# Batch 1 of a sparse attention with an MoE layer behind it: values of pairs 2 and 3 loaded ahead of rows of k and q, one stage for all block sums, and ScalarE's front reordered

## The chip, the cores and the metric

The kernel runs on one core of one Trainium2 chip. The metric is the device time of one execution in microseconds; lower is better. Inputs and output are float32 in device memory.

## The reference, cut to what matters

```python
B, H, S, D = 4, 8, 768, 64;  block, window = 32, 16;  nb = S // block   # 24 blocks
scale = 1 / sqrt(D)
k_sum = k.reshape(B, H, nb, block, D).max(axis=3)
v_sum = v.reshape(B, H, nb, block, D).mean(axis=3)
scores_l = scale * q @ k.T                      # masked to |i - j| < window
scores_s = scale * q @ k_sum.T + log(block)
a = softmax(concat([masked scores_l, scores_s]))
attn = a @ concat([v, v_sum])
x = attn.transpose(0, 2, 1, 3).reshape(B * S, H * D)          # 3072 x 512
h = x @ w_in                                                  # 512 -> 2048
out = (h / (1 + exp(-beta * h))) @ w_out                      # 2048 -> 512
```

Each query sees its neighbours at less than 16 positions, and one key and one value for each of the 24 blocks: the block's maximum of k and its mean of v.

## The kernel before, in words

**Tiles.** The eight heads go in four pairs, g = 0 to 3. Queries are taken in tiles of 64, two to a chunk of 128 rows (par 0 and 1), six chunks to a sequence. For a pair, `kw` holds the turned keys (for par 1 a copy shifted by 64) with the 24 block maxima in the columns from 96 on, `qt` the turned queries. `ve` holds the values shifted by 16 rows for par 0, `vo` the same values shifted by 64 more for par 1; the lowest 96 partitions of each are values, the upper 32 block means. One matmul thus gives the scores of a tile with its neighbours and all blocks; the scores are exponentiated on ScalarE (`attn`), multiplied with a band of ones on VectorE (`mask`), and multiplied with `ve` or `vo` on TensorE (`av`). A column of ones in the values gives the sum, by which VectorE divides (`norm`). The result is turned (`x_transpose`) into `xT`.

**The layer behind.** Units of tokens go through `h_group` (matmuls with `w_in` of k1 = 4 steps, then Silu with the scale beta on ScalarE) and `o_part` (matmuls with `w_out`, copied out by ScalarE, written by SyncE). Batch 0 is two units of 384 tokens, each later batch is one of 768.

**Order.** There is no planner with costs: each engine runs its instructions in the order in which the program issues them. Batch 0's attention is written out by hand and comes first (the front). Then, for each batch b, the list `main` holds the h groups and the output parts of batch b with times (1.3 and 0.865 each), and `side` holds the steps of attention of batch b + 1 with times given by `at_time`; `side` is sorted by time and merged into `main`. `up` is the time at which the output parts begin. The times only give an order.

**Loads.** GpSimd issues all loads from device memory, converting to bf16, in one queue: k and q of batch 0, its values, w_in, `load_run` of k and q of pairs 0 and 1 of batch 1, w_out (four parts), values of batch 1. Pairs 2 and 3 of batch 1 are loaded as rows (`load_row`: four DMAs for a pair) and turned by `cross`, two DMA transposes for a pair on SyncE's queue. Pairs 0 and 1 are turned on TensorE (`prep_k`, `prep_q`). `load_v(1, 2, 2)` and `load_v_edge(1, True)` bring the values of pairs 2 and 3. Each load there waits until the eighth load before it has landed.

**The gate.** Batch 2's loads (`load_next`) are issued on GpSimd behind `open_gate`, a memset of one small tile first by VectorE, then by GpSimd, which so waits until VectorE has come to that place.

**Block means.** `mean_v` sums the values with the matrix `A_avg` on TensorE: nine steps, each with one matmul for each pair, into 32 partitions per pair (`vm_ps`). A cast takes the sums to `vm` (in batch 0 to `vm_first`, on ScalarE), and `rows_v` spreads them on VectorE over the upper partitions of `ve` and `vo`. `copy_v` makes `vo` from `ve` by DMA on SyncE's queue or by a copy on VectorE or ScalarE.

**The front.** `av_first` multiplies the first half of a pair's scores with values (L412) and then with `vm_first` (L419). `fill` and `keep_warm` are matmuls without use on a bank of TensorE's; the bank `big` of the front also holds the turned beta, which `beta_copy` reads (L237). `fill_band` makes half of the band on ScalarE (L221); `x0` turns half of x, copied by ScalarE (L481). The activation of one element into `spare` (L614) brings ScalarE's table for Silu.

Lines of the profile: L341 block sums, L345 and L348 their casts, L354 `rows_v`, L329 `copy_v`, L303 and L305 the DMA transposes of `cross`, L311 and L313 batch 2's block maxima, L438 scores, L443 masks, L456 `av`, L465 and L466 `norm`, L501 and L508 the h groups, L522 output parts.

Of the kernel before, what the change touches and what calls it, by code (L numbers as in the profile page):

```python
# [12 lines left out]
def kernel(  # L13
# [10 lines left out]
    nc = tc.nc  # L24
# [5 lines left out]
    ACTF = mybir.ActivationFunctionType  # L30

    B, H, S, D = q.shape
# [4 lines left out]
    nch = S // P  # L37
# [36 lines left out]
    HM = nch // 2  # L74
# [39 lines left out]
    def load_v(b, g, n=1):  # L114
        lo, hi = PC * g + 1, min(PC * (g + n) + 1, HC)
        rows = v[b].rearrange("h s d -> (h s) d")
        src = rows[lo * P - W:hi * P - W].rearrange("(c p) d -> p c d", p=P)
        nc.gpsimd.dma_start(out=ve_bufs[b % 2][:, lo:hi, 0:D], in_=src)  # L118

    def load_v_edge(b, last):  # L120
        ve = ve_bufs[b % 2]
        rows = v[b].rearrange("h s d -> (h s) d")
        if last:
            nc.gpsimd.dma_start(out=ve[0:W, HC, 0:D], in_=rows[H * S - W:H * S])
        else:
            nc.gpsimd.dma_start(out=ve[W:P, 0, 0:D], in_=rows[0:P - W])
# [18 lines left out]
    warm = const.tile([P, 512], bf16, name="warm")  # L145
    spare = const.tile([P, 1], f32, name="spare")
# [71 lines left out]
    def fill_band(m0, m1):  # L218

        for par in range(2):  # L220
            nc.scalar.copy(out=band[:, par, m0:m1].rearrange("p m h f -> p (m h) f"),  # L221
                           in_=near[:, None].to_broadcast([P, 2 * (m1 - m0), QT]))
# [26 lines left out]
    def load_w_out(i, c=k2 // 4):  # L249
        nc.gpsimd.dma_start(out=w_out_sb[:, i * c:(i + 1) * c], in_=w_out_r[:, i * c:(i + 1) * c])  # L250
# [3 lines left out]
    at = {}  # L254
# [67 lines left out]
    def copy_v(b, g, m0=0, m1=nch, copy=None):  # L322
        ve = ve_bufs[b % 2][:, PC * g:PC * (g + 1) + 1]
        vo = vo_bufs[b % 2][:, PC * g:PC * (g + 1)]
        copies = copy if isinstance(copy, tuple) else (copy or nc.sync.dma_start,) * 2
        for (lo, n, at, d), move in zip(((D, D, 0, 0), (0, 32, D, 1)), copies):
            dst = vo[at:at + n].rearrange("p (h c) e -> p h c e", h=2)[:, :, m0:m1]
            src = ve[lo:lo + n, d:PC + d].rearrange("p (h c) e -> p h c e", h=2)[:, :, m0:m1]
            move(out=dst, in_=src)  # L329

    def fill(t, n):
        for _ in range(n):
# [237 lines left out]
    load_v_edge(1, False)  # L570
    load_v(1, 0, 2)
    load_w_out(3)
    for g in (2, 3):
        load_row("k", 1, g)
        load_row("q", 1, g)
    load_v(1, 2, 2)
    load_v_edge(1, True)

    for g in range(npair):
        open_scores(g, 0)  # L580
# [14 lines left out]
    for g in range(2):  # L595
        copy_v(0, g, 0, HM, dve)
        copy_v(0, g, HM, nch)
    mean_v(0, (0, 1), "t", act)
    av_first(0)()
    norm((0, 0, 0), HM)  # L600
    av_first(1, ps.tile([P, 2, 512], f32, name="av_ps", tag="big", bufs=3))()
    norm((0, 1, 0), HM)
    fill(big, 1)
    beta_copy()
    fill_band(HM, nch)
    x0(0, act)
    copy_v(0, 2, 0, HM, dve)
    copy_v(0, 3, 0, HM, (act, dve))
    for g in (2, 3):
        copy_v(0, g, HM, nch)  # L610
    fill(big, 1)
    mean_v(0, (2, 3), "big", act)
    x0(1, act)
    nc.scalar.activation(out=spare[:], in_=warm[:, 0:1], func=ACTF.Silu)  # L614
    av_first(2)()
    norm((0, 2, 0), HM)
    av_first(3, ps.tile([P, 2, 512], f32, name="av_ps", tag="big", bufs=3))()
# [12 lines left out]
    for b in range(B):  # L630
        us = [u for u, z in enumerate(units) if z[0] == b]
        up = sum(NG[u] for u in us) * GT
        total = up + nch * 4 * OT
        nxt = b + 1 if b + 1 < B else None
        pairs = tuple(range(npair))
        side = []

        def at_time(t, f, *a):
            side.append((t, lambda: f(*a)))

        if b == 0:
            for g in pairs:
                t = 2.0 + 2.0 * g
                at_time(t - 1.4, mask_half, g)
                at_time(t - 1.4, rows_v, 0, g, HM, nch)
                at_time(t, av, (0, g, 1), HM, HM, "t")
                at_time(t, norm, (0, g, 1), HM)
                at_time(t + 1.9, x_transpose, (0, g, 1), HM, HM, "t", dve)
            at_time(7.0, fill_band, 0, HM)
            at_time(7.0, band_edge, False)  # L650
            for n in range(k2):
                at_time(up - 7.5 + 0.4 * n, scale_w_out, n)
        if nxt == 1:
            first, step = up + 0.3, 4.4
            for g in pairs:
                t = first + step * g
                p = (up - 9.0, up - 4.5, up + 7.5, up + 8.6)[g]
                if g < 2:
                    at_time(p, prep_k, 1, g, "t")
                    at_time(p + 0.8, prep_q, 1, g, "t", dve)  # L660
                    at_time(p + 0.8, copy_v, 1, g)
                else:
                    at_time(up + 0.5, cross, 1, g)
                    at_time(up + 6.1 if g == 2 else first + step * 2 + 0.1, copy_v, 1, g, 0, nch, act)
                at_time(p, top_k, 1, g)
                at_time(p if g < 3 else first + step * 2 + 0.7, rows_k, 1, g)
                for par in range(2):
                    at_time(t, scores, 1, g, par)
                    at_time(t, mask, 1, g, par)
                if g % 2 == 0:  # L670
                    m = up + 1.0 if g == 0 else first + step * 2 + 0.5
                    at_time(m, mean_v, 1, (g, g + 1), "big")
                    for i in (g, g + 1):

                        at_time(m if i < 3 else first + step * 2 + 0.8, rows_v, 1, i)
                a = t + 3.5
                at_time(a, av, (1, g), 0, nch)
                at_time(a, norm, (1, g), nch)
                at_time(a + (0.1 if g < 2 else 2.9), x_transpose, (1, g), 0, nch, "big", dve)
        elif nxt is not None:  # L680
            for g in pairs:
                t = (0.65, 1.95, 5.85, 9.75)[g]
                at_time(0.1, copy_v, nxt, g)
                at_time(t, cross, nxt, g)
                m = 3.9 + 3.9 * g if g < 3 else up + 2.0
                at_time(m, max_k, nxt, g)
                at_time(m, rows_k, nxt, g)
            at_time(10.0, mean_v, nxt, pairs)
            for g in pairs:
                at_time(10.1 + 1.0 * g, rows_v, nxt, g)  # L690
            for g in range(npair + 1):
                t = up + 4.0 * g
                if g < npair:
                    for par in range(2):
                        at_time(t, scores, nxt, g, par)
                        at_time(t, mask, nxt, g, par)
                if g:
                    at_time(t, av, (nxt, g - 1), 0, nch)
                    at_time(t, norm, (nxt, g - 1), nch)
                    at_time(t, x_transpose, (nxt, g - 1), 0, nch, "big", dve)  # L700
        if nxt is not None:
            if nxt + 1 < B:
                def load_next(b, g):
                    if g == 0:
                        nc.vector.memset(ve_bufs[b % 2][SUM:P, 0:HC, D:VW], 1.0)
                        load_v_edge(b, False)
                    load_v(b, g)
                    if g == npair - 1:
                        load_v_edge(b, True)
                    load_row("k", b, g)  # L710
                    load_row("q", b, g)

                def open_gate():

                    nc.vector.memset(gate[:], 0.0)
                    nc.gpsimd.memset(gate[:], 0.0)

                if b == 0:
                    at_time(up + 7.0, open_gate)
                for g in pairs:  # L720
                    at_time(up + 7.1 + 0.1 * g if b == 0 else 1.0 + 4.5 * g, load_next, nxt + 1, g)
        main = []
        for j, u in enumerate(us):
            for i in range(NG[u]):
                ks = range(k1 - 1, k1) if j == 0 and i < 2 else range(k1)
                main.append(((j * NG[u] + i) * GT, lambda u=u, i=i, ks=ks: h_group(u, i, ks)))
        for j, u in enumerate(us):
            n = units[u][2] * HM
            main += [(up + (4 * (j * n + ms) + p) * OT, lambda u=u, ms=ms, p=p: o_part(u, ms, p, 4)) for ms in range(n) for p in range(4)]
        if nxt is not None:  # L730
            main += [(total + i, lambda i=i: h_group(us[-1] + 1, i, range(k1 - 1))) for i in range(2)]
        side.sort(key=lambda z: z[0])
        for t, f in main:
            while side and side[0][0] <= t:
                side.pop(0)[1]()
            f()
        for _, f in side:
            f()
# [30 lines left out]
```

## Time and profile before

| | us |
|---|---|
| median of 3 runs | 216.17 (215.77 to 216.43) |
| profiled execution, own time | 216.13 |
| its span | 214.3 |
| TensorE busy | 205.8 (96% of the span) |
| ScalarE busy | 118.7 (55%) |
| VectorE busy | 90.7 (42%) |
| GpSimd busy | 65.9 (31%) |
| TensorE's granted clock | 1.00 |

The span runs from the first to the last instruction; the own time of the execution holds what lies around it too. A busy share is an average over the stages, and matmuls are pipelined, so 96% does not mean that TensorE is at its peak. In the rows that are quoted, the first number is the start in us from the span's start, the second the time of the whole group in us; "xN" is the number of instructions, and brackets give the idle time of the engine before the group and who ended it. In rows of the chain of waits there is no bracket. In rows of DMA issues the last number is the time in us from issue to landing.

### The profile page before, as it was taken

How to read it: one execution, taken by the hardware profiler on the slowest of the kernel's cores; microseconds unless marked ns; L12 is line 12 of the kernel's file. 1: busy time of each engine (PE TensorE's matmuls, PEld its weight loads, DVE VectorE, ACT ScalarE, POOL GpSimd, SP SyncE). 2: the span in 40 equal slices, each digit the busy share in tenths (PEclk: the TensorE clock that was granted, in tenths of full speed). 3: DMA queues.
4: the chain of work that ended last, by engine and by line, in shares of the span. 5: the costliest groups of instructions: out<-in, count | busy, mean ns of one | idle time of the engine just before them, and what ended most of it. 6: DMA issues, size and time to landing. Idle time of an engine off the chain costs nothing.

```text
span 214.3 us, 4859 instructions
## 1 busy us (share of the span) xinstructions
PE 205.8 (96%) x2005; PEld 114.6 (53%) x2024; DVE 90.7 (42%) x233; ACT 118.7 (55%) x166; POOL 65.9 (31%) x88
## 2 busy tenths in 40 slices
PE   7998999999999999999999999999999999999992
PEld 3655666654455466564555465655554566654452
DVE  4676674497778310387644202814454000002121
ACT  3796867878476177578443286678342477740000
POOL 7983443343098971398630000000000000000000
PEclk9999999999999999999999999999999999999999
DMA  6999999999999999999999447721343400001222
GB/s 175 177 153 192 204 204 206 184 176 167 135 229 141 210 204 204 160 165 157 168 145 191 135 136 138 146 40 49 43 132 89 136 0 3 0 0 52 95 85 65
DMA packets 93622, 28.34 MB, mean 132 GB/s; under 512 B 82256, under 2 KB 90656, under 8 KB 93600
## 3 DMA queue, kind: packets, MB, share of 16 engines
q0 software_dynamic: 63184, 13.24, 76.2%
q1 hardware_dynamic: 29968, 14.26, 32.7%
q10 hardware_dynamic: 448, 0.52, 0.7%
q8 instruction: 16, 0.26, 0.5%
q14 instruction: 6, 0.05, 0.1%
HBM read 27.27 MB, written 6.29 MB: 157 GB/s over the span
## 4 chain that ended last, share of the span: by engine, by line
PE 93%; issue 2%; ACT 1%; DVE 1%; ACTq 0%
PE h_ps L501 39%; PE o_ps L522 39%; PE av_ps L456 4%; PE s_ps L438 3%; PE w_ps L552 2%; PE vm_ps L341 1%; PE pq L279 1%; PE pk L279 1%; PE s_ps L384 1%; PE av_ps L419 1%; PE px L480 1%; PE s_ps L379 1%; PE av_ps L412 1%; DVE km L293 0%; PE s_ps L367 0%
## 5 line engine op out<-in xcount | busy, mean ns | idle before, releaser
L501 PE MATMUL h_ps<-xT,w_in_sb 128*128 128x384 bf16 x512 | 86.2, 326 | 0.0
L522 PE MATMUL o_ps<-w_out_sb,h_sb 128*128 128x512 bf16 (+2 forms) x383 | 83.7, 370 | 2.2 <-issue 1.9
L508 ACT ACTIVATE h_sb<-h_ps,beta_sb 128x768 bf16<-128x768 f32 (+1 forms) x80 | 59.4, 771 | 24.5 <-PE h_ps L501 24.3
L501 PEld LDWEIGHTS <-w_in_sb 128*128 128x128 bf16 x512 | 49.1, 98 | 32.3 <-issue 0.2
L522 PEld LDWEIGHTS <-h_sb 128*128 128x128 bf16 x400 | 36.9, 98 | 40.6
L542 ACT COPY o_sb<-o_ps 128x512 f32<-128x512 f32 x18 | 10.5, 585 | 29.7 <-PE o_ps L522 17.4
L443 DVE TENSOR_TENSOR attn<-attn,band 128x768 bf16<-128x768 bf16 x24 | 13.4, 559 | 23.4 <-ACT attn L439 21.7
L439 ACT ACTIVATE attn<-s_ps 128x768 bf16<-128x768 f32 x24 | 18.1, 808 | 8.7 <-PE s_ps L438 8.6
L111 POOL DMA_DIRECT2D k_nat<-in_k_dram x20 | 16.8, 850 | 12.9 <-DMA kw<-k_nat 7.8
L542 DVE COPY o_sb<-o_ps 128x512 f32<-128x512 f32 x5 | 3.5, 692 | 38.5 <-PE o_ps L522 38.5
L111 POOL DMA_DIRECT2D q_nat<-in_q_dram x20 | 16.6, 840 | 7.9 <-DMA w_out_sb<-in_moe_w_out_dram 4.5
L466 DVE TENSOR_TENSOR x_nat<-av_ps,r 128x768 bf16<-128x768 f32 (+1 forms) x20 | 15.9, 798 | 0.7
L118 POOL DMA_DIRECT2D ve<-in_v_dram x12 | 14.4, 1196 | 5.5 <-DMA w_in_sb<-in_moe_w_in_dram 2.6
L311 DVE TENSOR_TENSOR half<-kw 128x384 bf16<-128x384 bf16 x8 | 2.9, 357 | 26.9 <-DMA kw<-k_nat 26.8
L293 DVE TENSOR_REDUCE km<-kw 128x24 bf16<-128x768 bf16 x8 | 7.6, 948 | 5.2 <-ACT kw L289 5.1
L456 PEld LDWEIGHTS <-attn 128*64 128x64 bf16 x336 | 6.7, 111 | 3.9 <-issue 2.3
L465 DVE RECIPROCAL r<-av_ps 128x12 f32<-128x12 f32 (+1 forms) x20 | 4.3, 215 | 10.5 <-PE av_ps L456 8.9
L456 PE MATMUL av_ps<-ve,attn 128*64 128x65 bf16 x168 | 8.5, 198 | 0.1
L456 PE MATMUL av_ps<-vo,attn 128*64 128x65 bf16 x168 | 8.3, 197 | 0.0
L438 PEld LDWEIGHTS <-kw 64*128 64x128 bf16 x288 | 4.9, 95 | 4.9 <-issue 4.1
L400 ACT ACTIVATE attn<-s_ps 128x768 bf16<-128x768 f32 x8 | 6.0, 808 | 0.7 <-PE s_ps L384 0.6
L552 PE MATMUL w_ps<-warm 128*128 128x512 bf16 x11 | 5.1, 632 | 1.3 <-DVE warm L156 1.3
(92 smaller groups left out, 143.9 us busy)
## 6 DMA issues: line engine op xcount, KB each, us to landing
out_dram<-o_sb SPq DMA_DIRECT2D x23, 256.0 KB, 2.3
w_out_sb<-in_moe_w_out_dram POOLq DMA_DIRECT2D x4, 512.0 KB, 17.1
k_nat<-in_k_dram POOLq DMA_DIRECT2D x20, 96.0 KB, 7.1
q_nat<-in_q_dram POOLq DMA_DIRECT2D x20, 96.0 KB, 7.2
w_in_sb<-in_moe_w_in_dram POOLq DMA_DIRECT2D x3, 512.0 KB, 14.4
ve<-in_v_dram POOLq DMA_DIRECT2D x6, 192.0 KB, 7.3
vo<-ve SPq DMA_DIRECT2D x10, 97.5 KB, 5.7
ve<-in_v_dram POOLq DMA_DIRECT2D x2, 384.0 KB, 13.2
```

The costliest lines, as they stand in the source:

```text
L111: nc.gpsimd.dma_start(out=t[:, :, h], in_=(k_row if nm == "k" else q_row)[b, g, :, h])
L118: nc.gpsimd.dma_start(out=ve_bufs[b % 2][:, lo:hi, 0:D], in_=src)
L438: nc.tensor.matmul(sv[:, h, m], kw[lo:lo + D, par, m, :], q[lo:lo + D, m, par], start=True, stop=True)
L439: nc.scalar.activation(out=a.rearrange("p m h f -> p h m f"), in_=sv, func=ACTF.Exp, scale=scale)
L443: nc.vector.tensor_mul(out=a, in0=a, in1=band[:, par])
L456: nc.tensor.matmul(ov[par * QT:(par + 1) * QT, h, m], a[:, par, m, h], t[:, PC * g + nch * h + m0 + m], start=True, stop=True)
L466: nc.vector.tensor_mul(out=x.rearrange("p m h d -> p h m d"), in0=ov[:, :, :, 0:D], in1=r[:, :, :, None].to_broadcast([P, 2, n, D]))
L501: nc.tensor.matmul(big[:, j, 0:MG], w_in_sb[:, ki, ni * P:(ni + 1) * P], xT[b][:, ki, tok:tok + MG], start=(ki == 0), stop=(ki == k1 - 1))
L508: nc.scalar.activation(out=hb.rearrange("p (k m) -> p k m", m=MG), in_=big[:, j:j + w, 0:MG], func=ACTF.Silu, scale=beta_sb[:, ni:ni + 1])
L522: nc.tensor.matmul(o_ps[:, c0:c1], h_bufs[(u, ni * w // k2)][:, ni % (k2 // w), ms * P:(ms + 1) * P], w_out_sb[:, ni, c0:c1], start=(ni == ...
L542: (nc.scalar.copy if u + 1 < len(units) else nc.vector.tensor_copy)(out=o_sb[:], in_=o_ps[:])
L552: nc.tensor.matmul(w_ps[:, 0], warm[:, 0:P], warm, start=True, stop=True)
```

## The change

- The loads of the values of pairs 2 and 3 of batch 1 are issued ahead of the eight row loads of k and q of these pairs, no longer behind them.
- The block sums of batch 1 are made in one stage for all four pairs (at `up + 2.6`), not in two stages of two pairs (at `up + 1.0` and at about `up + 9.6`). `rows_v` gets times of its own for each pair, and the `av` of pair 0 comes 0.8 later.
- ScalarE's copies `vo` of pairs 2 and 3 of batch 1 come at `up + 4.0` and `up + 6.1`, no longer at `up + 6.1` and about `up + 9.2`.
- The gate of batch 2's loads opens at `up + 8.5`, not at `up + 7.0`. On VectorE it so stands behind the norm of pair 1; before, it stood ahead of the block maxima of pair 2.
- In the front, `beta_copy` and the activation that brings the table move ahead of the first `av_first`; the band's second half moves behind the second turn of x; the copy `vo` of pair 3 is made wholly on VectorE (before, ScalarE made its first part), and the option of `copy_v` to give two engines goes.

```diff
     def copy_v(b, g, m0=0, m1=nch, copy=None):
...
-        copies = copy if isinstance(copy, tuple) else (copy or nc.sync.dma_start,) * 2
-        for (lo, n, at, d), move in zip(((D, D, 0, 0), (0, 32, D, 1)), copies):
+        for lo, n, at, d in ((D, D, 0, 0), (0, 32, D, 1)):
...
-            move(out=dst, in_=src)
+            (copy or nc.sync.dma_start)(out=dst, in_=src)
...
     load_w_out(3)
+    load_v(1, 2, 2)
+    load_v_edge(1, True)
     for g in (2, 3):
         load_row("k", 1, g)
         load_row("q", 1, g)
-    load_v(1, 2, 2)
-    load_v_edge(1, True)
...
     mean_v(0, (0, 1), "t", act)
+    beta_copy()
+    nc.scalar.activation(out=spare[:], in_=warm[:, 0:1], func=ACTF.Silu)
     av_first(0)()
     norm((0, 0, 0), HM)
     av_first(1, ps.tile([P, 2, 512], f32, name="av_ps", tag="big", bufs=3))()
     norm((0, 1, 0), HM)
     fill(big, 1)
-    beta_copy()
-    fill_band(HM, nch)
     x0(0, act)
-    copy_v(0, 2, 0, HM, dve)
-    copy_v(0, 3, 0, HM, (act, dve))
     for g in (2, 3):
+        copy_v(0, g, 0, HM, dve)
         copy_v(0, g, HM, nch)
     fill(big, 1)
     mean_v(0, (2, 3), "big", act)
     x0(1, act)
-    nc.scalar.activation(out=spare[:], in_=warm[:, 0:1], func=ACTF.Silu)
+    fill_band(HM, nch)
     av_first(2)()
...
-                    at_time(up + 6.1 if g == 2 else first + step * 2 + 0.1, copy_v, 1, g, 0, nch, act)
+                    at_time((up + 4.0, up + 6.1)[g - 2], copy_v, 1, g, 0, nch, act)
...
-                if g % 2 == 0:
-                    m = up + 1.0 if g == 0 else first + step * 2 + 0.5
-                    at_time(m, mean_v, 1, (g, g + 1), "big")
-                    for i in (g, g + 1):
-
-                        at_time(m if i < 3 else first + step * 2 + 0.8, rows_v, 1, i)
-                a = t + 3.5
+                at_time((up + 2.7, up + 2.7, up + 8.55, first + step * 2 + 0.8)[g], rows_v, 1, g)
+                a = t + (4.3 if g == 0 else 3.5)
...
+            at_time(up + 2.6, mean_v, 1, pairs, "big")
...
-                    at_time(up + 7.0, open_gate)
+                    at_time(up + 8.5, open_gate)
...
-                    at_time(up + 7.1 + 0.1 * g if b == 0 else 1.0 + 4.5 * g, load_next, nxt + 1, g)
+                    at_time(up + 8.5 + 0.01 * (g + 1) if b == 0 else 1.0 + 4.5 * g, load_next, nxt + 1, g)
```

## The prediction

> **What bounds the kernel now.** I read the page first, then the chain of waits, then the timelines of TensorE, ScalarE and VectorE in the two stretches that the change touches (18 to 24 us and 48 to 68 us), and last the DMA issues there.
>
> ```profile
> span 214.3 us, 4859 instructions
> ...
> PE 93%; issue 2%; ACT 1%; DVE 1%; ACTq 0%
> ```
>
> The chain that ends last is TensorE for 93% of the span. So only two things pay: less work on TensorE, or less waiting by it. Everything else counts only through what it makes TensorE wait for. The span is 214.3 us and the execution's own time 216.13, so 1.83 us lie around it, which the change does not touch. The runs' median is 216.17, 0.04 above; both are used as one below.
>
> The other engines hold 1% each of the chain. Their main piece is in the front:
>
> ```profile
> 19.36 0.82 ACT band L221 x2
> ...
> 20.59 0.52 ACT vo L329
> ...
> 21.12 0.27 ACT vm_first L345
> ...
> 22.38 0.76 PE h_ps L501 x4
> ```
>
> ScalarE copies the band, turns x, copies half of a vo, and only then casts the block sums of pair 2 (vm_first), on which TensorE waits. The timeline of TensorE shows the wait itself:
>
> ```profile
> 18.96 0.34 PE L480 MATMUL px<-identity,x_nat 128*128 128x128 bf16 x3 [0.19 <-DVE x_nat L466]
> 19.41 0.38 PE L333 MATMUL beta_ps<-warm 128*128 128x512 bf16 x1
> ...
> 21.43 0.34 PE L419 MATMUL av_ps<-vm_first,attn 32*128 32x65 bf16 x6 [0.44 <-ACT vm_first L345]
> ```
>
> **The change, front.** Beta's copy, the table load and the one-element activation move ahead of the first av; the band moves behind the second turn of x; ScalarE's vo copy goes to VectorE. ScalarE's timeline gives the prices:
>
> ```profile
> 17.39 0.54 ACT L345 CAST vm_first<-vm_ps 32x130 bf16<-32x130 f32 x2 [0.32 <-PE vm_ps L341]
> 19.18 0.17 ACT L237 COPY beta_sb<-beta_ps 128x16 f32<-128x16 f32 x1 [1.26 <-PE av_ps L419]
> ...
> 22.19 1.28 ACT L614 ACT_TABLE_LOAD   x1
> 23.48 0.20 ACT L614 ACTIVATE spare<-warm 128x1 f32<-128x1 bf16 x1
> ```
>
> The cast ends at 17.93. Beta's copy today comes after the fill in program order and waits for it, 1.26 us idle; moved up, it runs at once: 17.93 + 0.17 + 1.28 + 0.20 = 19.58. Then comes the first turn's copy (0.48 alone; its input is done at 19.30), to 20.06. TensorE's second block-sum group ends near 20.2, so the cast of pair 2 follows at about 20.2 to 20.45. TensorE needs it at 20.99 (21.43 less the 0.44 of idling). The wait of 0.44 is gone, with 0.5 us to spare. The fill at 19.41 no longer waits for beta's copy (ended 19.35) to stop reading its bank: the turn before it ends at 19.30, so another 0.11. The turn issues in about half its shown length, so that gap may be worth 0.28: the front gives 0.55, at most 0.72. The band's two copies (0.82) then run behind the second turn, to about 22.1; the first user is VectorE, after the norms of pairs 2 and 3.
>
> What could take the place of that wait is VectorE's four copies:
>
> ```profile
> 16.81 1.27 DVE L329 COPY vo<-ve 64x390 bf16<-64x390 bf16 x4 [1.68 <-DMA ve<-in_v_dram]
> ...
> 19.65 0.72 DVE L329 COPY vo<-ve 64x390 bf16<-64x390 bf16 x3
> ```
>
> Four copies instead of three: 19.65 + 1.27 = 20.92. Pair 3's av starts after pair 2's av and sums, at about 21.2 in the new order: 0.3 us of cover, nothing if the front gains its full 0.72. VectorE then waits for TensorE anyway (the norm of pair 2), so nothing else is late.
>
> **The change, block sums.** One group of all four pairs replaces two groups of two pairs. The chain of waits shows both kinds (some records of matmuls are missing, so the durations count, not the numbers of instructions):
>
> ```profile
> 50.84 0.51 PE vm_ps L341 x13
> 51.36 1.83 PE o_ps L522 x8
> ...
> 61.01 0.46 PE s_ps L438 x24
> ...
> 62.44 0.51 PE vm_ps L341 x11
> ...
> 86.26 0.52 PE vm_ps L341 x24
> ...
> 102.63 0.50 PE av_ps L456 x24
> ```
>
> Two pairs take 0.51 and again 0.51; four pairs, in batch 2, take 0.52. So 0.51 + 0.51 - 0.52 = 0.50 us of TensorE work goes. One cast of VectorE less is off the path. The later av of pair 0 (one output part later) reorders TensorE's work without adding any.
>
> Its condition: the values of pairs 2 and 3 must be there at about 52 us (50.84, less the front's 0.55, plus the eight output matmuls that now go ahead, the row of 1.83: 52.1). They are now issued right behind the last w_out and ahead of the eight row loads:
>
> ```profile
> 30.76 0.75 POOL L250 DMA_DIRECT2D w_out_sb<-in_moe_w_out_dram  x1 [1.09 <-DMA w_in_sb<-in_moe_w_in_dram]
> ...
> 47.44 0.82 POOL L111 DMA_DIRECT2D q_nat<-in_q_dram  x1 [1.09 <-DMA w_out_sb<-in_moe_w_out_dram]
> 48.25 1.51 POOL L118 DMA_DIRECT2D ve<-in_v_dram  x1
> ```
>
> ```profile
> w_out_sb<-in_moe_w_out_dram POOLq DMA_DIRECT2D x1, 512.0 KB, 16.4
> ```
>
> ```profile
> ve<-in_v_dram POOLq DMA_DIRECT2D x1, 368.0 KB, 12.0
> q_nat<-in_q_dram POOLq DMA_DIRECT2D x1, 96.0 KB, 6.0
> ...
> kw<-k_nat SPq DMA_TRANSPOSE x1, 8.6
> ...
> qt<-q_nat SPq DMA_TRANSPOSE x1, 9.6
> ```
>
> The last w_out lands at 30.76 + 16.4 = 47.2, the last of the eight rows at 47.44 + 6.0 = 53.4: 8 x 96 KB in 6.2 us, 124 KB per us. At that rate 368 KB take 3.0 us: landed at 50.2, 1.9 us early. Today the same load takes from 53.4 to 60.25 (48.25 + 12.0), 6.8 us; at that pace it would land at 54.0 and cost TensorE 1.9. I take 3.0, since the slow stretch today lies beside the transposes of k and q, which in the new order cannot start before the values are in.
>
> **The change, rows of k and q.** The rows land 3.0 us later, and SyncE's transposes wait for them:
>
> ```profile
> 48.52 1.31 SPq L303 DMA_TRANSPOSE kw<-k_nat  x1
> 50.43 1.21 SPq L305 DMA_TRANSPOSE qt<-q_nat  x1
> ```
>
> Pair 2's k was in place at 48.52 + 8.6 = 57.1, its q at 50.43 + 9.6 = 60.0. Its scores start at 61.01, after the change at 60.46. So there is almost no cover on q: at unchanged latencies it lands at 63.0, and TensorE stands for 2.5 us. The other end is a transpose with nothing beside it, in batch 3:
>
> ```profile
> kw<-k_nat SPq DMA_TRANSPOSE x1, 2.8
> ```
>
> With 2.8 both would be there long before 58. Which end is nearer? In the microsecond from 54 to 55 the two queues moved this:
>
> ```profile
> q0 software_dynamic: 1147, 0.15, 236.7%
> q1 hardware_dynamic: 32, 0.00, 4.7%
> ```
>
> While the values of pairs 2 and 3 came in (software queue, 0.15 MB), the transposes already issued moved next to nothing. That block of 3 us of values is now ahead of the transposes instead of among them. The rows behind the first transposes are as before, so I give each transpose its old time less these 3 us: k of pair 2 lands at about 57.1 again, q at about 60.0 or sooner. That leaves 0.4 us on q, and for k the maximum and two copies on VectorE (1.4 us) end before 60. Cost taken: 0; both ends stay in the range.
>
> The Trainium skill, page "DMA: Bandwidth & Descriptors", section "Queues, rings and completion order", says that each DMA engine takes one packet of each queue in turn. By that the transposes would have had an even share beside the values, and would gain nothing from their going first: 216.13 - 1.05 + 2.5 = 217.6. The row above speaks against even turns here.
>
> Behind the transposes in SyncE's queue stand the first output writes and the two transposes of x, which move later by as much as the last row does, about 3 us; x is used at 75.86 by the chain, so they are covered. ScalarE's vo copies of pair 2 no longer wait for values:
>
> ```profile
> 60.30 1.71 ACT L329 COPY vo<-ve 64x780 bf16<-64x780 bf16 x2 [1.86 <-DMA ve<-in_v_dram]
> ```
>
> **The change, the gate.** GpSimd starts batch 2's loads only when VectorE has cleared a gate, now behind the norm of pair 1:
>
> ```profile
> 57.89 0.07 DVE L715 MEMSET gate<- 1x16 f32 x1
> ...
> 60.35 0.96 DVE L466 TENSOR_TENSOR x_nat<-av_ps,r 128x768 bf16<-128x768 f32 x1
> ```
>
> That norm ends at 61.3, less 0.55: 60.8. The loads start 2.9 us later than at 57.9. Everything behind them on GpSimd and SyncE may move by up to 2.9: values of batch 2, their vo copies, k's transposes, then VectorE's maxima and block rows:
>
> ```profile
> 91.56 0.36 DVE L311 TENSOR_TENSOR half<-kw 128x384 bf16<-128x384 bf16 x1 [1.13 <-DMA kw<-k_nat]
> ...
> 98.88 0.35 DVE L354 COPY vo<-vm 32x780 bf16<-32x780 bf16 x1
> 100.38 1.26 DVE L443 TENSOR_TENSOR attn<-attn,band 128x768 bf16<-128x768 bf16 x2 [1.15 <-ACT attn L439]
> ```
>
> From 91.56 VectorE is busy to 99.23, then masks pair 0 (1.26), then TensorE may run its av, today at 102.63, after the change at 101.58. The mask would end at 99.23 + 1.26 + x = 100.49 + x, so a shift x above 1.1 stalls TensorE: from 0 to 1.8 us. I take 0, with x about 0.5: at 58 to 62 today the loads stand beside the transposes, which are nearly over when the new gate opens.
>
> **The sum.** 216.13 - 0.55 - 0.50 = 215.08, taken as 215.1. Own range: 214.7 (front 0.72 and some more in the stretches with less contention) to 215.5 (0.4 of small stalls).
>
> **The rivals.**
> 1. The transposes of k and q come late (slower). Place: TensorE before the scores of pair 2. Price: up to 2.5, so up to 217.6; k late also delays the gate. From a stall of 1.05 on, that is q landing after 61.5, the change loses. For it: only 0.4 us of cover. Against: the values no longer hold the engines. 217.6 is the time with unchanged latencies. Chance 0.17. The Trainium skill's rule of turns, cited above, would lead to this rival.
> 2. Batch 2 starts too late behind the gate. Place: the av of its pair 0. Price 0 to 1.8: 215.1 to 216.9; it loses from x = 2.15 on. For it: VectorE has 7.7 us of unbroken work there. Against: GpSimd's loads in between wait for DMAs, not only for their start. Chance 0.13.
> 3. The front does not give what it says: the four vo copies, or the table load, stand where vm_first stood. Then only 0.50 comes: 215.6. Chance 0.10.
>
> **How the numbers follow.** The forecast has 0.60. About 0.3% (0.65 us) is what a measurement of this kernel can tell from no change, so faster means below 215.5, slower above 216.8. Faster: most of the forecast's cases and little of the rivals, 0.55. Within: the rest of the forecast, rival 3, half of 2, a third of 1: 0.23. Slower: the worse part of 1 and of 2: 0.22. For 8 in 10 the range goes from 214.6 to 217.1, which takes in all of rivals 2 and 3 and most of 1.
>
> **What would show it.** Front right: no idle of TensorE before the L419 group of pair 2, the h groups start at 21.8 instead of 22.38. Block sums right: one vm_ps group of 0.52 near 52 us and none near 62, with no idle before it. Rows right: TensorE goes from output parts into the scores of pair 2 with no wait for a DMA or VectorE, near 60.4. Gate right: no wait before the av of batch 2's pair 0. It is wrong if an idle of over 0.5 us stands at one of these places, or if the stretch from 76 us on is longer than today.

## The result, and the profile after

| | median, us (lowest to highest, runs) | ratio to before, 95% interval |
|---|---|---|
| before, beside the first runs of the changed kernel | 216.46 (215.77 to 220.56, 22) | |
| changed | 215.64 (214.62 to 218.72, 22) | 0.9955 [0.9938, 0.9973] |
| changed, second comparison | 215.08 (214.11 to 218.05, 12) | 0.9928 [0.9894, 0.9962] |
| changed, third comparison | 215.19 (214.53 to 218.84, 12) | 0.9942 [0.9912, 0.9972] |

The changed kernel is faster by 0.45%, 0.97 us by the first ratio; the other two give 1.56 and 1.26. The runs of the changed kernel spread over more than the gain. The first profile of the changed kernel is of a slow execution of 218.72 us, so I read one of 214.53 us in its place and say where the two differ; a third profile is of 214.83 us. The page of the one of 214.53, to be held against the span of 214.3 and the 93% of before:

```profile
span 212.8 us, 4852 instructions
...
PE 92%; DMA 3%; issue 2%; DVE 1%; POOL 0%; POOLq 0%
```

TensorE is still the chain. (The 3% of DMA are the first loads; before, the chain was followed back there through warm-up matmuls.) The chain of waits of before, three rows that are not shown yet:

```profile
48.55 0.86 PE o_ps L522 x4
...
75.86 10.40 PE h_ps L501 x64
...
122.37 10.40 PE h_ps L501 x64
```

and the chain of the changed kernel (lines there: L340 block sums, L437 scores, L455 av, L500 h groups, L521 output parts):

```profile
21.66 0.76 PE h_ps L500 x4
...
47.77 0.86 PE o_ps L521 x4
...
51.78 0.52 PE vm_ps L340 x23
...
74.36 10.40 PE h_ps L500 x64
...
120.87 10.40 PE h_ps L500 x64
```

Read the starts as stations. The first h groups start at 21.66 for 22.38, so the front has brought 0.72. The output parts of batch 0 start at 47.77 for 48.55, 0.06 more. Batch 1's h groups start at 74.36 for 75.86: another 0.72, from the stretch with the block sums, where one vm_ps group of 0.52 stands for two. Batch 2's h groups start at 120.87 for 122.37: the same 1.50, so nothing was given back in this execution. Own time: 216.13 to 214.53, 1.60.

The front on ScalarE and VectorE:

```profile
18.01 0.17 ACT L237 COPY beta_sb<-beta_ps 128x16 f32<-128x16 f32 x1
18.20 1.28 ACT L599 ACT_TABLE_LOAD   x1
19.49 0.20 ACT L599 ACTIVATE spare<-warm 128x1 f32<-128x1 bf16 x1
...
20.12 0.54 ACT L344 CAST vm_first<-vm_ps 32x130 bf16<-32x130 f32 x2
...
21.06 0.93 ACT L221 COPY band<-near 128x384 bf16<-128x384 bf16 x2
```

```profile
19.65 1.31 DVE L328 COPY vo<-ve 64x390 bf16<-64x390 bf16 x4
```

and on TensorE:

```profile
18.63 0.39 PE L332 MATMUL beta_ps<-warm 128*128 128x512 bf16 x1
...
18.98 0.34 PE L479 MATMUL px<-identity,x_nat 128*128 128x128 bf16 x3
19.46 0.58 PE L340 MATMUL vm_ps<-ve,A_avg 128*32 128x130 bf16 x14
...
20.57 0.36 PE L418 MATMUL av_ps<-vm_first,attn 32*128 32x65 bf16 x6
20.85 0.22 PE L411 MATMUL av_ps<-ve,attn 96*64 96x65 bf16 x1
21.02 0.19 PE L411 MATMUL av_ps<-vo,attn 96*64 96x65 bf16 x1
...
21.59 0.82 PE L500 MATMUL h_ps<-xT,w_in_sb 128*128 128x384 bf16 x4
```

and, from TensorE's timeline of before, the block sums of pairs 2 and 3 in the front:

```profile
19.72 0.58 PE L341 MATMUL vm_ps<-ve,A_avg 128*32 128x130 bf16 x14
```

ScalarE does what was forecast, to 0.1 us. Before, TensorE came from the start of the turn (18.96, shown in the prediction) to these block sums in 0.76 us; now it does so in 0.48 (18.98 to 19.46). Before, the fill at 19.41 started only when beta's copy had ended (19.35), and I put the 0.28 down to that wait. (Both kernels have one fill ahead of the turn and one behind it, and each profile has a record of only one of the two, 19.41 before and 18.63 after; no fill has moved.) One thing goes beyond the forecast of 0.55: the first matmul with vo of pair 3 starts at 21.02, 0.06 behind the end of VectorE's fourth copy (19.65 + 1.31 = 20.96), 0.17 behind the one with ve that was issued before it: TensorE now waits a little for VectorE's copies.

The rows of k and q of pairs 2 and 3, in the DMA issues from 51 to 58 us (medians of two), and what SyncE's queue, TensorE and VectorE did:

```profile
kw<-k_nat SPq DMA_TRANSPOSE x2, 4.1
qt<-q_nat SPq DMA_TRANSPOSE x2, 3.2
```

```profile
51.91 1.92 SPq L303 DMA_TRANSPOSE kw<-k_nat  x1
54.19 1.22 SPq L305 DMA_TRANSPOSE qt<-q_nat  x1
```

```profile
60.06 0.52 PE L437 MATMUL s_ps<-qt,kw 64*128 64x64 bf16 x24
60.74 2.54 PE L521 MATMUL o_ps<-w_out_sb,h_sb 128*128 128x512 bf16 x11 [0.16 <-issue]
```

```profile
57.08 0.95 DVE L293 TENSOR_REDUCE km<-kw 128x24 bf16<-128x768 bf16 x1
...
60.36 0.07 DVE L709 MEMSET gate<- 1x16 f32 x1
```

The medians mix two pairs. Taken one by one, pair 2's k took 5.1 us, for 8.6 before, and its q 3.6, for 9.6; pair 3's took 3.0 and 2.8, for 8.7 and 7.4. The transposes of pair 2 start 3.4 and 3.8 us later, and yet its k lands at 51.91 + 5.1 = 57.0, where VectorE takes it up at once (57.08), and its q at 54.19 + 3.6 = 57.8. The scores need them at 60.06 and wait for nothing (no bracket). The gate opens at 60.36.

Batch 2 is where executions of one kernel differ. SyncE's rows in the execution of 214.53:

```profile
75.22 8.97 SPq L328 DMA_DIRECT2D vo<-ve  x8
84.30 1.23 SPq L303 DMA_TRANSPOSE kw<-k_nat  x1
```

and in the one of 218.72, with VectorE and TensorE:

```profile
75.16 11.01 SPq L328 DMA_DIRECT2D vo<-ve  x8
86.28 2.80 SPq L303 DMA_TRANSPOSE kw<-k_nat  x1
```

```profile
99.99 0.36 DVE L311 TENSOR_TENSOR half<-kw 128x384 bf16<-128x384 bf16 x1 [2.56 <-DMA kw<-k_nat]
```

```profile
104.00 0.22 PE L455 MATMUL av_ps<-ve,attn 128*64 128x65 bf16 x1 [2.54 <-DVE attn L442]
```

The eight vo copies of batch 2 stand ahead of the transposes of k in SyncE's queue. The last one waits for the values of pair 3; when these come late, the transposes go late, VectorE gets pair 2's k late, masks late, and the av of batch 2's pair 0 stands for 2.54 us. Before, the first transpose was issued at 82.47; after, at 84.30, 85.64 and 86.28 in three profiles.

### The profile page after: what moved, and what is told of

The parts are those of the page before. It is cut to its first block, busy times and chain, and to the rows that moved or that the text cites. A ratio compares the mean times of both kernels' runs of the same rounds, so it can differ in the third digit from the quotient of the medians.

```text
span 217.0 us, 4852 instructions
## 1 busy us (share of the span) xinstructions
PE 204.2 (94%) x2005; PEld 113.4 (52%) x2024; DVE 90.0 (41%) x233; ACT 118.3 (55%) x165; POOL 66.0 (30%) x88
## 4 chain that ended last, share of the span: by engine, by line
PE 77%; DMA 14%; issue 3%; DVE 3%; ACT 1%; POOL 1%; SPq 0%; POOLq 0%
PE h_ps L500 33%; PE o_ps L521 31%; DMA kw<-k_nat 5%; DMA ve<-in_v_dram 4%; PE av_ps L455 3%; DMA q_run<-in_q_dram 3%; DMA out_dram<-o_sb 2%; PE s_ps L437 2%; PE vm_ps L340 1%; PE pq L279 1%; PE pk L279 1%; PE s_ps L383 1%; PE px L479 1%; DVE x_nat L465 1%; PE s_ps L378 1%
## 5 line engine op out<-in xcount | busy, mean ns | idle before, releaser
L500 PE MATMUL h_ps<-xT,w_in_sb 128*128 128x384 bf16 x512 | 86.3, 326 | 0.0
L521 PE MATMUL o_ps<-w_out_sb,h_sb 128*128 128x512 bf16 (+2 forms) x383 | 83.6, 370 | 2.1 <-issue 1.7
L500 PEld LDWEIGHTS <-w_in_sb 128*128 128x128 bf16 x512 | 49.1, 98 | 32.3 <-issue 0.2
L521 PEld LDWEIGHTS <-h_sb 128*128 128x128 bf16 x400 | 37.0, 98 | 40.9
L455 PE MATMUL av_ps<-ve,attn 128*64 128x65 bf16 x168 | 8.7, 198 | 3.3 <-DVE attn L442 2.5
L455 PEld LDWEIGHTS <-attn 128*64 128x64 bf16 x336 | 6.8, 111 | 7.6 <-DVE attn L442 3.0
L455 PE MATMUL av_ps<-vo,attn 128*64 128x65 bf16 x168 | 8.3, 197 | 0.3 <-DVE attn L442 0.3
L437 PEld LDWEIGHTS <-kw 64*128 64x128 bf16 x288 | 4.9, 95 | 4.5 <-issue 4.0
L437 PE MATMUL s_ps<-qt,kw 64*128 64x64 bf16 x288 | 6.3, 191 | 0.0
```

Source lines behind the costliest of these rows:

```text
L437: nc.tensor.matmul(sv[:, h, m], kw[lo:lo + D, par, m, :], q[lo:lo + D, m, par], start=True, stop=True)
L455: nc.tensor.matmul(ov[par * QT:(par + 1) * QT, h, m], a[:, par, m, h], t[:, PC * g + nch * h + m0 + m], start=True, stop=True)
L500: nc.tensor.matmul(big[:, j, 0:MG], w_in_sb[:, ki, ni * P:(ni + 1) * P], xT[b][:, ki, tok:tok + MG], start=(ki == 0), stop=(ki == k1 - 1))
L521: nc.tensor.matmul(o_ps[:, c0:c1], h_bufs[(u, ni * w // k2)][:, ni % (k2 // w), ms * P:(ms + 1) * P], w_out_sb[:, ni, c0:c1], start=(ni == ...
```

## The experiments

All are compared with the kernel before, run beside them; a profile is of one execution, and its own time stands beside the median where the two differ.

### One part at a time

The changed kernel was run again beside them.

> The changed kernel as it is, for a profile to stand beside the others and a time on the same chip. Both theories: 215.1 to 215.7. The gate theory expects in the profile a wait of TensorE of some 0.5 to 1 us before the av of pair 0 or 1 of batch 2, ended by VectorE's mask; its rival none there.

The front alone on the kernel before:

```diff
     mean_v(0, (0, 1), "t", act)
+    beta_copy()
+    nc.scalar.activation(out=spare[:], in_=warm[:, 0:1], func=ACTF.Silu)
...
-    beta_copy()
-    fill_band(HM, nch)
     x0(0, act)
-    copy_v(0, 2, 0, HM, dve)
-    copy_v(0, 3, 0, HM, (act, dve))
     for g in (2, 3):
+        copy_v(0, g, 0, HM, dve)
         copy_v(0, g, HM, nch)
...
-    nc.scalar.activation(out=spare[:], in_=warm[:, 0:1], func=ACTF.Silu)
+    fill_band(HM, nch)
```

> The kernel before with the new order of the front alone. Theory: TensorE's wait for vm_first and the fill's wait for beta's copy are all there is to win in the front, and all later stages keep their old loads, so the h groups start at 21.6 instead of 22.4 and the time falls by 0.78 us to about 215.4, or 215.6 if only 0.55 comes. Rival: a start that is earlier by 0.8 only brings TensorE sooner to a wait for w_in, w_out or batch 1's rows, and the time stays within 0.2 us of before.

And the changed kernel with the old front, the same diff the other way round:

> The changed kernel with the old order of the front: loads, block sums, vo copies of batch 1 and the gate are new. Theory: one vm_ps group less is worth 0.50 us, smoother DMA of pairs 2 and 3 up to 0.3 more, and the later gate takes back some 0.8, so 216.0 to 216.5, no change that can be measured. Rival: the gate costs nothing, then 215.4 to 215.7.

Measured: front alone 216.01 (214.72 to 218.33, 12 runs), ratio 0.9961 [0.9927, 0.9995]; all but the front 216.02 (215.22 to 219.87, 12 runs), 0.9963 [0.9933, 0.9993]; both 0.9928 [0.9894, 0.9962]. Each half is faster than before, and 0.39% + 0.37% = 0.76% is near what both together show beside them (0.72%), though each of these has an interval of about 0.3 points to either side. The profile of the changed kernel (214.83) has no wait of TensorE in front of the av of batch 2's pairs 0 and 1 among its listed waits, as the rival of the gate theory had it. The stations say where the time went, in the chains of waits:

| | first h groups | batch 1's h groups | stretch | batch 2's h groups | stretch |
|---|---|---|---|---|---|
| before | 22.38 | 75.86 | 53.48 | 122.37 | 46.51 |
| front alone | 22.30 | 75.72 | 53.42 | 123.30 | 47.58 |
| all but the front | 22.23 | 75.00 | 52.77 | 122.37 | 47.37 |
| changed, 214.53 | 21.66 | 74.36 | 52.70 | 120.87 | 46.51 |
| changed, 214.83 | 21.57 | 74.27 | 52.70 | 121.10 | 46.83 |

The stretch between the first two stations is shorter by 0.65 to 0.78 wherever the block sums are in one stage, and only there. The stretch in batch 2 is 46.51 at its best and up to 1.1 longer, also in the front alone, whose loads and gate are those of before. There the list of TensorE's waits shows it (us in all, times, longest):

```profile
PE av_ps L456 <- DVE attn L443: 0.8, 2, 0.5
```

So the loss in batch 2 does not need the moved gate. With the gate opened at 57.74 as before, the values of batch 2's pair 3 were issued at 75.89 in that execution, for 73.53 before, after waits for other loads.

### The front's pieces

The band back ahead of the first turn of x, in a single run (217.89 us), read for its front alone:

```diff
+    fill_band(HM, nch)
     x0(0, act)
...
     x0(1, act)
-    fill_band(HM, nch)
     av_first(2)()
```

> The changed kernel with the band's copies of 0.82 us back ahead of the first turn's copy on ScalarE. Theory: ScalarE's order alone decides the front; the first turn's copy then ends at 20.9, TensorE's av of pair 2 starts 0.5 us later and the h groups start at 22.1 instead of 21.5. Rival: the front's gain comes from beta's fill alone, then 21.6.

```profile
19.67 0.91 ACT L221 COPY band<-near 128x384 bf16<-128x384 bf16 x2
20.49 0.47 ACT L480 COPY xT<-px 128x384 bf16<-128x384 bf16 x1
20.98 0.54 ACT L344 CAST vm_first<-vm_ps 32x130 bf16<-32x130 f32 x2
```

The turn's copy comes late, TensorE waits 0.6 us for it in front of the av, the cast is at 20.98, near the 21.12 of before, and the h groups start at 22.20. And ScalarE's part of pair 3's vo put back, again a single run (215.2 us):

```diff
...
+    copy_v(0, 2, 0, HM, dve)
+    copy_v(0, 3, 0, HM, (act, dve))
     for g in (2, 3):
-        copy_v(0, g, 0, HM, dve)
         copy_v(0, g, HM, nch)
```

> The changed kernel with the first part of pair 3's vo copy back on ScalarE (0.52 us), between the first turn's copy and the casts. Theory: the cast of pair 2 then ends at 20.9 instead of 20.5, TensorE waits 0.2 for it and the h groups start at 21.8. Rival: the four copies on VectorE were the tighter end in the changed kernel, then the start stays at 21.5.

```profile
20.41 0.52 ACT L329 COPY vo<-ve 64x390 bf16<-64x390 bf16 x1
20.96 0.54 ACT L345 CAST vm_first<-vm_ps 32x130 bf16<-32x130 f32 x2
```

TensorE waits 0.25 for that cast, and the h groups start at 22.14. The executions reach the front at different times, so I count from the start of VectorE's vo copies, with the h groups' start from TensorE's timeline:

| | vo copies start | they take | h groups start | from the copies' start to the h groups |
|---|---|---|---|---|
| before | 19.65 | 0.72 (three) | 22.31 | 2.66 |
| all but the front | 19.57 | 1.08 (three) | 22.16 | 2.59 |
| band back | 19.72 | 1.32 | 22.20 | 2.48 |
| ScalarE's vo back | 19.98 | 0.80 (three) | 22.14 | 2.16 |
| front alone | 19.99 | 1.62 | 22.23 | 2.24 |
| changed, 214.53 | 19.65 | 1.31 | 21.59 | 1.94 |
| changed, 214.83 | 19.50 | 1.37 | 21.50 | 2.00 |
| changed, 218.72 | 19.64 | 1.22 | 21.53 | 1.89 |

The whole front is worth 0.66 to 0.77 in the changed kernel's three profiles, counted against before. The band's place is most of it: with it back, 0.18 is left. ScalarE's vo copy is the smaller part: 0.16 to 0.27 against these three, and less than nothing against the front alone, whose four copies took 1.62. In every profile of the new front that keeps four copies and the band's new place, the h groups start 0.62 to 0.68 after the last copy ends. Where TensorE's matmuls stand apart (by 0.17 in the execution of 214.53, 0.22 in that of 214.83), VectorE's copies set the end of the front. In the execution of 218.72 the first matmuls with ve and vo of pair 3 both start at 20.93, so there TensorE did not wait for the copies.

### The order of the loads

The changed kernel with the rows of k and q ahead of the values again, and one stage of block sums all the same:

```diff
     load_w_out(3)
-    load_v(1, 2, 2)
-    load_v_edge(1, True)
     for g in (2, 3):
         load_row("k", 1, g)
         load_row("q", 1, g)
+    load_v(1, 2, 2)
+    load_v_edge(1, True)
```

> The changed kernel with the values of pairs 2 and 3 of batch 1 loaded behind the rows of k and q again; the one stage of block sums stays near 52 us. Theory: the values land at 60, so the block sums stop TensorE from 52 to about 60; some 7 to 8 us more in the first part, less what later stages get back because batch 2's loads are then on time: 220 to 223. Rival: the transposes were what held the values up, so the values land at 56 and TensorE waits only 4: 218 to 219.

Measured: 226.49 (225.08 to 227.19, 4 runs), ratio 1.0458 [1.0417, 1.05]. The waits of TensorE, the chain, and the DMA issues from 51 to 58 us:

```profile
PE vm_ps L340 <- DMA ve<-in_v_dram: 9.5, 2, 9.1
```

```profile
48.41 12.76 DMA ve<-in_v_dram
61.22 0.94 PE vm_ps L340 x26
```

```profile
qt<-q_nat SPq DMA_TRANSPOSE x2, 9.2
kw<-k_nat SPq DMA_TRANSPOSE x1, 9.1
```

The values land at 48.41 + 12.8 = 61.2, TensorE needs them at 51.8 and stands 9.1 us, and the transposes take what they took before or longer (pair 2's 8.9 and 10.4). So the load order is the condition of the one stage, and it is also what makes the transposes fast. The time is above the 220 to 223 that was expected, since the loss is more than the wait. Against the execution of 214.53, the profile's own 226.61 is 12.1 more: the block sums start 9.4 later; the stretch from them to batch 1's h groups takes 24.29 (61.22 to 85.51) for 22.58, with a granted clock of 0.50 from 61 to 64 us and block sums of 0.94 for 0.52; and batch 2's stretch takes 0.9 more.

### The gate

Opened earlier, and the loads behind it at their old times; and opened later:

```diff
-                    at_time(up + 8.5, open_gate)
+                    at_time(up + 7.0, open_gate)
...
-                    at_time(up + 8.5 + 0.01 * (g + 1) if b == 0 else 1.0 + 4.5 * g, load_next, nxt + 1, g)
+                    at_time(up + 7.1 + 0.1 * g if b == 0 else 1.0 + 4.5 * g, load_next, nxt + 1, g)
```

> The changed kernel with the gate of batch 2's loads at its old place, ahead of the block maximum of pair 2. Theory: the gate's place is what takes back part of the gain, through batch 2's values and transposes, so with the old place the runs gather near the fastest of the changed kernel, 214.6, with 0.6 to 0.8 us less than the changed kernel in the same series. Rival: the gate guards the transposes of batch 1's k and q; opened at 57 us it lets loads in beside them, the scores of pair 2 wait, and the time is the changed kernel's or up to 1.5 us above it.

```diff
-                    at_time(up + 8.5, open_gate)
+                    at_time(up + 11.0, open_gate)
...
-                    at_time(up + 8.5 + 0.01 * (g + 1) if b == 0 else 1.0 + 4.5 * g, load_next, nxt + 1, g)
+                    at_time(up + 11.0 + 0.01 * (g + 1) if b == 0 else 1.0 + 4.5 * g, load_next, nxt + 1, g)
```

> The changed kernel with the gate of batch 2's loads later still, behind VectorE's second copy of block rows of pair 3, some 4 us after its new place. Theory: the old place brought nothing (the loads from there on are bound by the transfers), but a start 4 us later is past that cover: batch 2's values land 2 to 4 us later, block sums and av of batch 2 wait, and the time is 217 to 219. Rival: the start has no weight at all, then the changed kernel's time within 0.5 us.

Measured: early 215.32 (214.76 to 217.61, 12 runs), ratio 0.9953 [0.9919, 0.9987], beside 0.9928 [0.9894, 0.9962] of the changed kernel: the intervals overlap, and the 0.6 to 0.8 us that were expected did not come. Late 217.66 (216.56 to 221.2, 12 runs), 1.0047 [1.0017, 1.0078], beside 0.9942 [0.9912, 0.9972] of the changed kernel: 2.5 us slower. Three rows of GpSimd in the early kernel:

```profile
57.32 0.10 POOL L710 MEMSET gate<- 1x16 f32 x1 [4.78 <-DVE gate L709]
...
75.58 1.64 POOL L111 DMA_DIRECT2D q_nat<-in_q_dram  x2 [3.61 <-DMA ve<-in_v_dram]
77.20 1.07 POOL L118 DMA_DIRECT2D ve<-in_v_dram  x1
```

The gate opens 3.2 us sooner than in the changed kernel (57.32 for 60.51), and yet the values of pair 3 are issued at 77.20, later than its 74.91: in between GpSimd stood 3.61 us until an earlier load had landed. In that execution (217.61) TensorE even waited 1.3 us for them at batch 2's block sums. What the gate's move costs is therefore not measurable here. The late gate (its profile an execution of 220.59) shows the other side: the first transpose at 87.50, a wait of 1.1 us for the values at batch 2's block sums, and 2.5 us of waits in front of its av. So a start 4 us later is paid for, and one 3 us sooner brings nothing.

### The queue in front of batch 2's transposes

If the last vo copies hold the transposes back, they can be put behind, or taken off the queue. Pair 3's copies behind the transposes of pairs 0 and 1:

```diff
-                at_time(0.1, copy_v, nxt, g)
+                at_time(2.5 if nxt == 2 and g == 3 else 0.1, copy_v, nxt, g)
```

> The changed kernel with one change of order on SyncE's queue: batch 2's vo copy of pair 3 is issued behind the transposes of pairs 0 and 1 of batch 2, not ahead of them. Theory: the transposes stand in the queue behind a copy that waits for the last values (85 us in the profile); they could start at 81, and the maxima, block rows and masks of batch 2 with them, so the waits before the av go and the time is 214.4 to 214.9, with fewer runs above 216. Rival: the transposes are bound by the transfers that are under way, so they start earlier and end as late: no change beside the changed kernel.

All of batch 2's vo copies on VectorE:

```diff
-                at_time(0.1, copy_v, nxt, g)
+                at_time((0.1, 0.1, 0.1, 7.7)[g] if nxt == 2 else 0.1, copy_v, nxt, g, 0, nch, dve if nxt == 2 else None)
```

> The changed kernel with batch 2's vo made by copies on VectorE, which is idle from 76 to 90 us, not by DMAs. That takes eight transfers, 0.59 MB, out of the stretch where batch 2's loads and transposes are late, and frees SyncE's queue for the transposes. Theory: if transfers in this stretch take back what the change gains, the time falls to 214.3 to 214.8 and the fastest runs are no faster than the changed kernel's fastest. Rival: TensorE's waits come from elsewhere, or VectorE becomes late by its eight copies (3.4 us): 215.4 or more.

The copies of pairs 0 to 2 on VectorE, pair 3's left ahead of the transposes:

```diff
-                at_time(0.1, copy_v, nxt, g)
+                at_time(0.1, copy_v, nxt, g, 0, nch, dve if nxt == 2 and g < 3 else None)
```

> The changed kernel with batch 2's vo of pairs 0 to 2 made by VectorE; pair 3's stays a DMA of SyncE ahead of the transposes, so that these still begin only when all values are in. Theory, as the last two runs left it: transposes and loads slow each other when they run side by side, so the transposes must stay behind the values, but 0.44 MB less of copies lets the values land 1 to 2 us sooner; 214.4 to 214.9, fewer runs above 216, and no wait for values or masks in the profile. Rival: the stretch is bound by the loads themselves, then as the changed kernel, 215.1 to 215.4.

The changed kernel again, beside the first two of these and the late gate:

> The changed kernel as it is, beside the next three on the same chip. All theories: 215.1 to 215.6.

| | median, us (lowest to highest, runs) | ratio to before |
|---|---|---|
| changed, beside the next two | 215.19 (214.53 to 218.84, 12) | 0.9942 [0.9912, 0.9972] |
| pair 3's copies behind | 217.5 (216.21 to 219.75, 12) | 1.005 [1.002, 1.0079] |
| all on VectorE | 215.88 (214.58 to 221.73, 12) | 0.9962 [0.9933, 0.9992] |
| pairs 0 to 2 on VectorE (without the changed kernel beside it) | 215.01 (214.21 to 216.27, 11) | 0.9942 [0.9917, 0.9967] |

With pair 3's copies behind, the transposes do go sooner, and from pair 1's on they come later (SyncE, then VectorE; profile of 216.21):

```profile
79.05 1.43 SPq L303 DMA_TRANSPOSE kw<-k_nat  x1
80.65 1.28 SPq L305 DMA_TRANSPOSE qt<-q_nat  x1
82.11 3.67 SPq L303 DMA_TRANSPOSE kw<-k_nat  x1
```

```profile
93.41 0.36 DVE L311 TENSOR_TENSOR half<-kw 128x384 bf16<-128x384 bf16 x1 [4.07 <-DMA kw<-k_nat]
```

Issued at 82.11, pair 1's k is there at 93.4; in the execution of 214.53 it was issued at 87.00 and VectorE took it up at 91.99. The DMA issues from 60 to 96 us give a median of 9.0 for k's transposes, for 5.3 there, and TensorE waits 1.3 us for batch 2's masks. That theory fell: the place of the copies was not a stall to be taken away; it held the transposes back until the values were in. With all copies on VectorE the transposes run among the loads from 74.81 on, with 9.3, and now the values pay (execution of 218.40):

```profile
PE vm_ps L340 <- DMA ve<-in_v_dram: 2.4, 1, 2.4
```

Behind this wait the granted clock was 0.50 from 87 to 90 us, and the block sums took 0.92. The ratio's interval overlaps with the changed kernel's, so this loss is shown for that execution and not for the median.

With pair 3's copies left as the guard, the transposes begin at 84.56, take 4.9, and TensorE waits for nothing in batch 2. The values were expected 1 to 2 us sooner; the transposes that wait for them began no sooner than in the best profile (84.30). The median equals the changed kernel's within the intervals. Its highest run is 216.27, where the changed kernel's three sets of runs reach 218.05 to 218.84, but the changed kernel did not run beside it, so I do not call it better. No version was shown to beat the changed kernel.

## Why the prediction was right, point by point

**Front: 0.55, at most 0.72.** Right in mechanism; the upper size came. The wait for vm_first is gone, and the fill's wait was worth the 0.28 of the upper count, not 0.11. Measured 0.72 at the first h groups and 0.66 to 0.77 by the count from VectorE's copies. The step that failed is the cover of 0.3 on these copies: they end at 20.96, as forecast (20.92), but TensorE came for them sooner, so there is no cover left, and it waits about 0.2 in two of the three profiles. The prediction named this as rival 3 and as "nothing if the front gains its full 0.72". In the front alone the copies took 1.62, and the front gained only 0.42 (2.66 to 2.24).

**Block sums: 0.50.** One group of 0.52 near 52, none near 62, no idle before it, and the forecast's 0.50 by the durations. (They are seven steps and not nine, as the description of the kernel had it: the rows show 14 matmuls for two pairs.) The stretch from the first h groups to batch 1's is shorter by 0.78, though. Of the 0.28 beyond the 0.50, 0.06 lie ahead of the output parts; behind their start, the chain has 0.11 less in gaps named "issue" and 0.10 less in the output parts themselves (20.99 for 21.09). Why these are shorter is not shown.

**Values of pairs 2 and 3 at 50.2.** Issued at 32.92, landed after 17.3: 50.2.

```profile
32.92 1.48 POOL L118 DMA_DIRECT2D ve<-in_v_dram  x1 [1.66 <-DMA k_run<-in_k_dram]
```

They were issued while w_out was still coming, so the time from issue to landing is long, but the sum from the rows' rate gave the right time of landing. TensorE needed them at 51.8, so 1.6 us are left.

**Rows of k and q: k at 57.1, q by 60.0.** Right for k, which lands at 57.0, and too careful for q, which lands at 57.8. Pair 2's transposes lost not the 3.0 us of the values but 3.5 and 6.0. Rival 1 (217.6 from unchanged latencies) did not come; the kernel with the old load order shows 8.9 and 10.4 for these two, so it is the values ahead of them that made the difference. The rule of the Trainium skill, page "DMA: Bandwidth & Descriptors", section "Queues, rings and completion order", that each engine takes a packet of each queue in turn, led the prediction to unchanged latencies as its rival 1. As it was read there, neither these runs nor pair 3's copies put behind (9.0 among the loads, 5.3 after them) bear it out.

**Gate: 60.8, shift x of 0.5 against a threshold of 1.1.** The gate opens at 60.36. The step that failed is the size of the shift, not the threshold. The first transpose of batch 2 goes 1.8, 3.2 and 3.8 us later in the profiles of 214.53, 214.83 and 218.72, and VectorE starts the masks of pair 0 at 99.10, 100.21 and 103.39, for the 99.23 from which the prediction counted. So x is -0.1, 1.0 and 4.2, and TensorE loses nothing, 0.3 and 2.5 us at this place. In the best, the transposes themselves were faster (a median of 5.3 for 6.3), so VectorE's second maximum starts at 91.99 for 91.56, and the mask comes in time. In the one of 218.72 rival 2 came, at the place and by the chain that it named. The other profiles with pair 3's copies ahead of the transposes fit this. With the first transpose at 82.47, 84.30 and twice 84.56, the stretch in batch 2 is 46.51; at 85.64 it is 46.83; at 86.00 and 86.10 it is 47.58 and 47.37; and from 86.28 to 87.60, in four profiles, TensorE waits 1.1 to 2.8 us in all for the masks. The late gate confirms that lateness there is paid for. But the cause is not the gate alone, as the prediction had it: the front alone, with the old gate, loses 1.07 in the same stretch, and the early gate brought no gain.

**The sum.** Forecast 0.55 + 0.50 = 1.05, or 215.1. Measured up to batch 1's h groups 0.72 + 0.78 = 1.50, from which batch 2 takes back nothing to some us, by execution. The median change of 0.97 in the first comparison is thus not the forecast's sum come true but a larger gain less part of it. Held against the 1.50 of one pair of profiles, about 0.5 is given back there, 0.2 in the third and nothing in the second; that is a difference of medians and one profile, an estimate. That 0.97 came so near to 1.05 is partly luck: the gain up to batch 1's h groups was over 0.4 larger than forecast, and a loss in batch 2, which the forecast had put at nothing, stood against it. What makes the values of batch 2 land sooner or later from execution to execution stays open.

## What to carry to other kernels

When DMA transposes and loads share the DMA engines, order them: loads that are needed first go first, and a copy that waits for the last load can be a useful guard in front of the transposes. A stage that packs twice the work into the same matmul time pays if its inputs can be had; test that by putting the loads back. And after a wait of the critical engine has gone, look at once for the next producer with little cover, on the spot and one batch later.

## What the runs showed of the hardware that was not expected

- A DMA transpose of k of pairs 2 and 3 took 8.6 to 9.1 us beside the loads of values, 5.1 and 3.0 behind them; one of q 7.4 to 10.4, and 3.6 and 2.8. Issued 5 us sooner, among loads, pair 1's k of batch 2 landed later (93.4, for 92.0 at the latest).
- Starting loads 3.2 us sooner brought the last of them no sooner (issued at 77.20 for 74.91, in one profile each).
- The same four vo copies on VectorE took 1.21 to 1.62 us from one execution to the next. GpSimd was issuing DMAs in the same microseconds both where they took 1.21 and where they took 1.62, so that alone does not tell the two apart; the cause stays open.
- Block sums of four pairs took 0.52 us where two pairs took 0.51.
- Behind waits of TensorE of 9.1 and 2.4 us the granted clock was 0.50 for over 3 us more (old load order; all copies on VectorE). Behind the late gate's wait of 2.2 us it was 0.66 from 105 to 108 us, and behind the 2.5 us in the execution of 218.72 it was 1.00, so the length of the wait alone does not tell.
- The table load took 1.28 us, and the next activation started 0.01 us behind it (18.20, 19.49), as in the old place. The Trainium skill, page "ScalarE: Activation LUTs", section "What ACT_TABLE_LOAD costs", has the same 1283 ns and another 1380 ns of drain for a switch; no such drain stands behind the load here.
